# The RMS norm between two expert layers on 128x3 root elements, and one group of weight maxima read earlier

## The chip, the cores and the metric

The kernel runs on one core of a Trainium2 chip. A core has a matrix engine (TensorE: PE in the profile, its weight loads are PEld), a vector engine (VectorE: DVE), an activation engine (ScalarE: ACT), GpSimd (POOL) and SyncE (SP), whose queue issues nearly all DMAs here. PE writes to PSUM, which has eight banks of 128 x 512 fp32. The metric is device time in microseconds (us); lower is better.

## The reference

```python
x = attention(q, k, v)                    # (4,8,576,64), blocks of 64, block-causal, softmax
x = x.transpose(0, 2, 1, 3).reshape(2304, 512)
h = x @ w_in                              # 512 -> 2048
x = softplus(h) @ w_out                   # 2048 -> 512      first expert layer
rms = sqrt(mean(x * x, axis=-1) + 1e-6)   # one number for each token
xn = x / rms * rms_g
g = xn @ w_gate                           # 512 -> 1536
out = (g * sigmoid(g) * (xn @ w_val)) @ w_out2   # second expert layer
```

Inputs and outputs are fp32. The change concerns `rms` and, apart from it, the largest magnitude of `w_gate`/`w_val`, which the kernel needs for a scale of its fp16 products.

## The kernel before, in words

**Layout.** The 2304 tokens are cut into NB = 6 blocks of BLK = 384. Activations are held transposed: features on the 128 partitions (KD = 4 groups of 128), tokens along the free axis. So the mean over a token's 512 features runs over partitions and over four groups.

**Stages.** Attention units (batch, query group, head pair) run for each block, and their PE work is mixed with the first expert layer (phase A: `g1` and `g2` with hidden groups 0 to 8 of 16, for all blocks). The last attention work ends at about 350 us. Phase B (about 355 to 565 us) runs hidden groups 9 to 15 for all blocks in the order 4, 5, 0, 1, 2, 3 and, at the end of each block, `evac_b`: the four result banks are added to the partial result (line 1086), squared and summed over the four groups, and the norm's root is computed. Phase C (from 565 us) is the second expert layer: `g34` (gate and value products in seven fp16 block products, each in three passes) and `g5`.

**The root (lines 1088 to 1110).** ACT squares four tiles of 128x384, DVE adds them into `acc`. PE multiplies by a matrix of ones (line 1097), so that the token sums stand on every partition, 384 columns wide. From there all is 128x384: DVE scales the sums (line 1099); ACT loads a table set, takes Ln and then Exp with factor -0.5 (lines 1102 to 1104); the next activation loads its own set again. One Newton step on DVE follows, four operations (the three products in `pair2`, line 1080, and line 1109). The last two blocks evacuated (2 and 3 in token order; the fifth and the sixth below) are normalised at once (`direct`). The other four store the 128x384 root to DRAM (line 1114), and `load_xn` reads it back in phase C beside the block.

**The norm itself (`norm_x`).** DVE multiplies each of four tiles by `rms_g` and by the root `rs` (line 1126); then ACT and DVE split and combine quarters of the block into seven fp16 pairs (lines 1131, 1132, 1080).

**The maxima.** `top_unit` loads 512 KB of raw weights twice for each unit and DVE takes the largest magnitude of each (line 544). For the first eight gate/value units (16 loads, 8 MB) that happens before phase B's own weights are converted, after the seven units of w1 that phase B needs. `scales` turns maxima into a power of two with one small fp32 PE product of the form that spreads a column over all partitions (line 561: the column, broadcast, as weights; the identity `id_b` as the moving side) and some 128x1 DVE operations.

**What sets the order.** Nothing is scheduled at run time. `Plan` collects every operation with a key, an estimated duration and its dependences, simulates the engines twelve times, keeps the best round and emits all instructions in that order. Each engine then runs its queue in order; so does SP, where a load that waits for its buffer holds back every DMA behind it. Buffers come from rings: raw weights use `R_wraw` (two buffers) in attention and, from phase B's weights on, also `R_m` (two more). In attention SP's queue also carries the transposes of the probabilities (line 868, `pt<-pst`), which the product with V waits for.

Of the kernel before, what the change touches and what calls it, by code (L numbers as in the profile page):

```python
# [312 lines left out]
def t_mm16(n):  # L313
    return n * 0.4167e-3
# [46 lines left out]
def kernel(  # L361
# [71 lines left out]
    rs_dram = {j: dram.tile([128, BLK], FP32, name=f"rsd{j}") for j in range(NB)}  # L433
# [9 lines left out]
    R_r = Ring(pool_at(1), 3, [128, BLK], FP32, "r")  # L443
# [6 lines left out]
    def mm(o, l, r, start, stop, **kw):  # L450
        nc.tensor.matmul(o, lhsT=l, rhs=r, start=start, stop=stop, **kw)  # L451
# [60 lines left out]
    fac_b = R_fac.new()  # L512
    R_id = Ring(pool_at(1), 1, [128, 128], FP32, "id")
# [563 lines left out]
    rs_op = []  # L1077

# [3 lines left out]
    def evac_b(j, key, direct):  # L1082
# [23 lines left out]
        rs_op[:] = [op("ACT", 2 * t_act(BLK) + 2.56, key, root, [ms], [rs])]  # L1106
        pair2(key, t, rs, rs, ALU.mult, [rs], [t])
        pair2(key, t, t, ms, ALU.mult, [t, ms], [t])
        op("DVE", t_dve2(BLK), key, lambda: nc.vector.tensor_scalar(t(), t(), -0.5, 1.5, ALU.mult, ALU.add), [t], [t])
        pair2(key, rs, rs, t, ALU.mult, [rs, t], [rs])  # L1110
        if direct:
            norm_x(j, y, rs, key)
            return
        op("SP", 0.45, key, lambda: nc.sync.dma_start(out=rs_dram[j], in_=rs()), [rs], [("rsd", j)], done=1.0, nbytes=196608)


    def load_xn(j, key):
        t, rs = R_y.new(), R_r.new()
        load(key, t, y_dram[j], reads=[("yd", j, d) for d in range(KD)], writes=[(t, d) for d in range(KD)], nbytes=786432)
        load(key, rs, rs_dram[j], reads=[("rsd", j)], writes=[rs], nbytes=196608)  # L1120
        norm_x(j, t, rs, key)

    def norm_x(j, t, rs, key):
        x = x_b[j] = R_x.new()
        for k in range(KD):
            op("DVE", t_dve(BLK, True), key + 4, lambda k=k: nc.vector.scalar_tensor_tensor(t()[:, k], t()[:, k], gvec[:, k:k + 1], rs(), ALU.mult, ALU.mult), [(t, k), rs, "gvec"], [(t, k)], port=True)  # L1126
# [28 lines left out]
    def g34(j, i, key, first):  # L1155
# [41 lines left out]
        op("ACT", t_act(BLK, False) + 0.09 + (1.28 if first else 0.0), key + 2, lambda: nc.scalar.activation(e1(), ps(A)(), ACTF.Silu, scale=fac(3, sd)), [A, ("f", 3, sd)], [e1], after=rs_op + sp_op[-1:] if first else ())  # L1197
# [165 lines left out]
    R_fac.before = list(att_ops)  # L1363
    R_id.before = list(att_ops)
    op("DVE", 0.1, when(3 * per_block), lambda: nc.vector.memset(ones, 1.0), [], ["eye", "ones"])
    op("DVE", 0.1, win[NB - 1] - 6, lambda: nc.vector.memset(fac_b(), 0.0), [], [fac_b])
    load(win[NB - 1] - 6, id_b, eye, writes=[id_b], nbytes=65536)
    t_b = win[NB] + LAG * step
# [4 lines left out]
    for i in range(N_GV[0]):  # L1373
        top_unit(("gv", i), win[NB - 1] + 6 + 5 * (NF1 - NA) + 2 * i)
    scales(win[NB], 2, 0, scale_x)
    scales(win[NB], 0, 0, None)
# [146 lines left out]
```

## Time and profile before

| | us |
|---|---|
| time, median of 3 runs | 968.07 (964.41 to 977.81) |
| time of the profiled execution | 966.15 |
| its span | 964.4 |
| PE busy | 944.7 (98%) |
| PEld busy | 837.2 (87%) |
| DVE busy | 740.9 (77%) |
| ACT busy | 624.8 (65%) |
| DMA, mean | 156 GB/s, 150.83 MB |

The span runs from the first to the last instruction of the profiled execution; its time is 1.75 us longer. Busy time is the union of an engine's instructions, and a matmul's end is modelled, so for the cost of a matmul in a stream one reads the distance between starts, not its duration. An fp32 matmul stands in the trace as two passes, each with its own weight load. The granted TensorE clock is full speed (2.4 GHz) in every slice of the span.

### The profile page before, as it was taken

The numbers are of one execution on the slowest core, as the hardware profiler recorded it, in microseconds if no ns is written. First come the engines' busy times: TensorE is split into PE (matmuls) and PEld (weight loads), VectorE is DVE, ScalarE is ACT, GpSimd is POOL, SyncE is SP. The second block draws the span as 40 slices with busy tenths as digits, with TensorE's granted clock in tenths as the row PEclk, the third lists the DMA queues.
The fourth block names the chain that finished last, engine by engine and source line by source line (L and its number), as shares of the span: only waits on it lengthen the run. The fifth ranks groups of instructions, "written<-read, shape, count | busy, mean of one in ns | idle before, by whom it ended". The sixth has DMA issues, their size and how long they took to land. (4 is left out here: it accounts for less than half of the span.)

```text
span 964.4 us, 19849 instructions
## 1 busy us (share of the span) xinstructions
PE 944.7 (98%) x7592; PEld 837.2 (87%) x7592; DVE 740.9 (77%) x1689; ACT 624.8 (65%) x1406; POOL 51.4 (5%) x220
## 2 busy tenths in 40 slices
PE   7998999999999999999999999999999999999998
PEld 5797899999999999999999997777888778877885
DVE  6999998887988849579898789977877744455455
ACT  7999798886888859356898556545664633433332
POOL 1000211120121100000000000000000000000000
PEclk9999999999999999999999999999999999999999
DMA  8656767965667447977864751424130200135312
GB/s 281 189 163 203 195 161 165 221 166 152 157 150 153 108 152 251 366 272 290 284 224 161 239 164 31 153 109 165 47 110 1 78 22 13 56 129 184 136 67 88
DMA packets 128926, 150.83 MB, mean 156 GB/s; under 512 B 86464, under 2 KB 101312, under 8 KB 127296
## 3 DMA queue, kind: packets, MB, share of 16 engines
q1 hardware_dynamic: 128256, 143.29, 48.6%
q0 software_dynamic: 576, 6.29, 1.8%
q8 instruction: 59, 0.97, 0.4%
q14 instruction: 35, 0.29, 0.1%
HBM read 99.22 MB, written 29.88 MB: 134 GB/s over the span
## 5 line engine op out<-in xcount | busy, mean ns | idle before, releaser
L451 PE MATMUL b<-x,w 128*128 128x192 f16 (+1 forms) x4176 | 484.5, 272 | 3.3 <-ACT m L1188 3.3
L451 PEld LDWEIGHTS <-w 128*128 128x128 f16 x3024 | 250.6, 98 | 12.6 <-issue 4.4
L451 PE MATMUL b<-g,w 128*128 128x384 f32 x1152 | 227.9, 339 | 0.0
L451 PEld LDWEIGHTS b<-x,w 128*128 128x128 f32 x1152 | 200.2, 188 | 3.6 <-issue 0.6
L451 PEld LDWEIGHTS b<-g,w 128*128 128x128 f32 x1152 | 199.7, 188 | 2.5 <-issue 0.5
L451 PE MATMUL b<-w,g 128*128 128x512 f16 (+1 forms) x654 | 145.6, 377 | 0.0
L451 PEld LDWEIGHTS <-g 128*128 128x128 f16 x654 | 63.5, 98 | 67.8
L1176 DVE TENSOR_TENSOR m<-m 128x384 f32<-128x384 f32 x72 | 40.0, 555 | 74.7 <-ACT m L1188 73.8
L1188 ACT COPY m<-b 128x384 f32<-128x384 f32 x108 | 50.8, 477 | 69.0 <-PE b L451 68.5
L799 DVE TENSOR_REDUCE nm<-b 128x1 f32<-128x288 f32 (+8 forms) x160 | 70.4, 450 | 20.9 <-PE b L451 20.0
L836 ACT ACTIVATE P<-b,nm 128x288 f32<-128x288 f32 (+8 forms) x160 | 79.5, 499 | 6.4 <-DVE nm L799 4.0
L451 PE MATMUL b<-khl,qbd 128*128 128x448 f32 (+7 forms) x360 | 68.7, 310 | 1.1 <-DVE t L1030 0.8
L344 ACT CAST g<-t 128x384 fp32r<-128x384 f32 x96 | 48.9, 513 | 25.7 <-PE b L451 22.8
L862 DVE SCALAR_TENSOR_TENSOR pst<-P,nm,pst 128x64 f16<-128x64 f32 (+8 forms) x108 | 58.1, 544 | 4.4 <-ACT pst L859 3.7
L451 PEld LDWEIGHTS b<-khl,qbd 128*128 128x128 f32 x360 | 57.9, 188 | 3.4 <-DVE t L1030 1.1
L354 DVE TENSOR_TENSOR g<-t,g 128x384 fp32r<-128x384 f32 x96 | 52.6, 552 | 8.7 <-ACT g L344 8.6
L859 ACT ACTIVATE pst<-P,nm 128x576 f16<-128x576 f32 (+8 forms) x75 | 41.7, 569 | 9.9 <-DVE nm L845 5.3
L1197 ACT ACTIVATE t<-b,fac 128x384 f32<-128x384 f32 x36 | 20.9, 579 | 36.3 <-PE b L451 36.3
L844 POOL TENSOR_SCALAR nm<-nm 128x1 f32<-128x1 f32 (+1 forms) x120 | 31.8, 265 | 223.5 <-ACT P L836 167.0
L1212 ACT CAST g<-t 128x384 f16<-128x384 f32 x36 | 18.4, 511 | 36.8 <-DVE t L1211 36.8
L1174 DVE TENSOR_TENSOR m<-b,m 128x384 f32<-128x384 f32 x72 | 39.8, 553 | 2.3 <-PE b L451 2.3
L1023 ACT ACTIVATE t<-b 128x384 f32<-128x384 f32 x51 | 24.7, 487 | 25.3 <-PE b L451 23.7
(139 smaller groups left out, 1208.5 us busy)
## 6 DMA issues: line engine op xcount, KB each, us to landing
wraw<-in_w2gv_dram SPq DMA_DIRECT2D x33, 512.0 KB, 4.1
wraw<-in_w_dram SPq DMA_DIRECT2D x25, 512.0 KB, 3.9
wraw<-in_w2o_dram SPq DMA_DIRECT2D x16, 512.0 KB, 4.8
qf<-in_qP_dram SPq DMA_DIRECT2D x42, 192.0 KB, 3.1
m<-in_w2gv_dram SPq DMA_DIRECT2D x15, 512.0 KB, 6.1
y<-yd SPq DMA_DIRECT2D x10, 768.0 KB, 6.4
xd<-x SPq DMA_DIRECT2D x32, 192.0 KB, 3.7
x<-xd POOLq DMA_DIRECT2D x4, 1536.0 KB, 8.4
```

Source lines behind the costliest of these rows:

```text
L344: "ACT": ("ACT", t_act(n), lambda: nc.scalar.copy(dst(), src())),
L354: "DVE": ("DVE", t_dve(n), lambda: nc.vector.tensor_tensor(dst(), a(), b(), ALU.subtract)),
L451: nc.tensor.matmul(o, lhsT=l, rhs=r, start=start, stop=stop, **kw)
L799: aop("DVE", t_dve(cn), key, lambda sp=sp, col=col, cn=cn: nc.vector.tensor_reduce(nm()[:, col:col + 1], sp()[:, :cn], axis=AX.X, op=ALU.m ...
L836: aop("ACT", 0.24 + cn * 0.836e-3, key, lambda sp=sp, col=col, c0=c0, cn=cn: nc.scalar.activation(P()[:, c0:c0 + cn], sp()[:, :cn], ACTF.E ...
L844: small(("POOL",), lambda e: e.tensor_scalar(nm()[:, 4 + i0:4 + i1], nm()[:, 4 + i0:4 + i1], 1e-9, 1.0 if whole(u) else 2.0**-14, ALU.add, ...
L859: "ACT": ("ACT", t_act(n) + 0.09, lambda: nc.scalar.activation(hi(), pc(), ACTF.Copy, scale=r())),
L862: aop("DVE", t_dve(n, True), key, lambda: nc.vector.scalar_tensor_tensor(lo(), pc(), r(), hi(), ALU.mult, ALU.subtract), [P, (nm, "r", ib) ...
L1023: op("ACT", t_act(BLK, False) + (1.28 if not sp_op else 0.0), key - 5, lambda: nc.scalar.activation(e(), h()[:, :BLK], ACTF.Softplus), [h] ...
L1174: op("DVE", t_dve(BLK), k, lambda: nc.vector.tensor_tensor(dst(), a(), b(), alu), rd, wr, port=o_sb(rd))
L1176: op2([("DVE", t_dve(BLK), lambda: nc.vector.tensor_tensor(dst(), a(), b(), alu)), ("POOL", t_pool2(BLK), lambda: nc.gpsimd.tensor_tensor( ...
L1188: op("ACT", t_act(BLK, False), key + 1, lambda o=o, s=s: nc.scalar.copy(s(), ps(o)()), [o], [s])
```

## The change

1. **Token sums.** The product ones x `acc` (384 columns) becomes three products with `acc` as weights (128 tokens each) and one column of ones as the moving side. The sums then stand with tokens on partitions: 128 x 3 numbers for a block.
2. **Root.** On 128x3: a first guess by integer shift (DVE) and subtraction from a constant (one small ACT operation), then three Newton steps of three DVE operations each. No Ln, Exp or table load is left. The results of all blocks stay in one small tile, `rt`.
3. **Spread.** `norm_x` has PE spread the roots: three products of the form of line 561, into a PSUM bank, and DVE's four multiplications read the root from that bank. The store and reload of the root through DRAM are gone.
4. **Maxima.** The first eight gate/value units are loaded and reduced during attention, gated on `g1` products of blocks 2 to 4, in the two `R_wraw` buffers; the two scales that follow are due earlier.
5. The first Silu no longer has to come after the last root; ring `R_r` shrinks from 3 to 2 buffers.

```diff
-        op("PE", 0.65, key, lambda: mm(o()[:, :BLK], ones, acc(), True, True), [acc, "ones"], [o], cols=t_mm16(2 * BLK))
-        ms, rs, t = R_r.new(), R_r.new(), R_r.new()
-        op("DVE", t_dve(BLK), key, lambda: nc.vector.tensor_scalar(ms(), o()[:, :BLK], 1.0 / DM, 1e-6, ALU.mult, ALU.add), [o], [ms])
-        def root():
-            nc.scalar.preload_act_table_set("natural_log_exp_and_others")
-            nc.scalar.activation(rs(), ms(), ACTF.Ln)
-            nc.scalar.activation(rs(), rs(), ACTF.Exp, scale=-0.5)
...
+        def sums():
+            for c in range(NT):
+                mm(o()[:, c:c + 1], acc()[:, 128 * c:128 * c + 128], ones[:, 0:1], True, True)
+        op("PE", 0.25 * NT, key, sums, [acc, "ones"], [o], cols=t_mm16(128))
+        root(j, o, key)
...
+        dve(lambda: v.tensor_scalar(m(), o()[:, 0:NT], 1.0 / DM, 1e-6, ALU.mult, ALU.add), [o], ["rm"])
+        dve(lambda: v.tensor_scalar(t().bitcast(U32), m().bitcast(U32), 1, None, ALU.logical_shift_right), ["rm"], ["rt"])
+        op("ACT", 0.1, key, lambda: nc.scalar.activation(y().bitcast(I32), t().bitcast(U32), ACTF.Copy, scale=-1.0, bias=float(0x5F3759DF)), ["rt", rt_b], [cell])
+        for _ in range(3):
+            dve(lambda: v.scalar_tensor_tensor(t(), y(), -0.5, m(), ALU.mult, ALU.mult), [cell, "rm"], ["rt"])
+            dve(lambda: v.tensor_tensor(t(), t(), y(), ALU.mult), ["rt", cell], ["rt"])
+            dve(lambda: v.scalar_tensor_tensor(y(), t(), 1.5, y(), ALU.add, ALU.mult), ["rt", cell], [cell])
...
+        def spread():
+            for c in range(NT):
+                mm(o()[:, 128 * c:128 * c + 128], rt_b()[:, 3 * j + c:3 * j + c + 1].to_broadcast([128, 128]), id_b(), True, True)
+        op("PE", 0.109 * NT, key + 3, spread, [("root", j), id_b, rt_b] + [(t, k) for k in range(KD)], [o], cols=t_mm16(2 * BLK))
...
+    for i in range(N_GV[0]):
+        top_unit(("gv", i), win[3] + (win[NB] - win[3]) * i / N_GV[0], [[g1_op[steps[20 + 3 * i]]], [g1_op[steps[21 + 3 * i]]]])
+    scales(win[NB - 1], 2, 0, scale_x)
+    scales(win[NB - 1], 0, 0, None)
```

**Order on PE, end of phase B.** First PE's queue around the fifth block's token sum, before (`g,w` are second-layer products of the first expert, `x,w` first-layer products; `r` is `acc`):

```order
L451 MATMUL b_7363<-g,w 128x384 x3
L451 MATMUL b_7370<-g,w 128x384 x3
L451 MATMUL b_7375<-r,ones 128x384
L451 MATMUL b_7381<-x,w 128x384 x12
L451 MATMUL b_7351<-g,w 128x384 x3
L451 MATMUL b_7359<-g,w 128x384 x3
```

And the same place after the change (`rt` holds the roots, `id` is the identity):

```order
L450 MATMUL b_7401<-ones,r 128x1 x3
L450 MATMUL b_7405<-g,w 128x384 x3
L450 MATMUL b_7411<-g,w 128x384 x3
L450 MATMUL b_7417<-x,w 128x384 x12
L450 MATMUL b_7390<-g,w 128x384 x3
L450 MATMUL b_7397<-g,w 128x384 x3
L450 MATMUL b_7456<-id,rt 128x128 x3
L450 MATMUL b_7405<-g,w 128x384 x3
```

The one product became three, and 24 matmuls later PE's own queue now holds three products that wait for the finished root; before, PE waited for no root directly.

**Order on DVE, same place, after the change.** DVE's queue in the second half of the fifth block's root, from the second Newton step on; rows of other work stand between (`g<-t,g` belongs to the first expert, `w<-wg,fac,w` and `wg<-wg` convert weights):

```order
L1120 TENSOR_TENSOR rt<-rt 128x3
L354 TENSOR_TENSOR g<-t,g 128x384
L1121 SCALAR_TENSOR_TENSOR rt<-rt 128x3
L589 SCALAR_TENSOR_TENSOR w<-wg,fac,w 128x256
L1119 SCALAR_TENSOR_TENSOR rt<-rt 128x3
L589 SCALAR_TENSOR_TENSOR w<-wg,fac,w 128x512
L1120 TENSOR_TENSOR rt<-rt 128x3
L354 TENSOR_TENSOR wg<-wg 128x2x128
L1121 SCALAR_TENSOR_TENSOR rt<-rt 128x3
```

The five operations of 128x384 that stood in this stretch before are gone, and eleven of 128x3 stand in their place, the last five of them between four pieces of other work.

**Order on SP, in attention, after the change.** SP's queue where the first maxima are loaded, block 2's attention (`xd` stores x, `yd` stores partial results, `qf` loads queries):

```order
L464 DMA wraw<-in_w2gv_dram 128x512
L1058 DMA yd_84<-y 128x384
L870 DMA_TRANSPOSE pt<-pst 128x8x128
L1066 DMA xd_79<-x 128x384 x2
L464 DMA wraw<-in_w2gv_dram 128x512
L1058 DMA yd_84<-y 128x384 x2
L464 DMA qf_110<-in_qP_dram 128x384
L870 DMA_TRANSPOSE pt<-pst 128x8x128
```

The two loads of `wraw` are new here: before, no weight load stood between the transposes of this stretch. Sixteen such loads now stand there.

## Rows read from the trace of the kernel before

**Rows 1.** The page: span, busy time of the engines.

```profile
span 964.4 us, 19849 instructions
PE 944.7 (98%) x7592; PEld 837.2 (87%) x7592; DVE 740.9 (77%) x1689; ACT 624.8 (65%) x1406; POOL 51.4 (5%) x220
```

**Rows 2.** Windows: stretch, length, PE, PEld, DVE, ACT, POOL busy, clock, DMA share, GB/s.

```profile
0.00:40.00 40.00, 32.37 (x273) 24.43 (x274) 30.69 (x83) 32.08 (x95) 4.03 (x27) 1.00 0.74 247
75.00:150.00 75.00, 70.74 (x559) 64.31 (x560) 70.11 (x205) 65.81 (x180) 13.37 (x50) 1.00 0.68 184
...
225.00:300.00 75.00, 75.00 (x610) 71.42 (x609) 65.59 (x195) 61.11 (x168) 11.52 (x49) 1.00 0.64 157
...
560.00:590.00 30.00, 28.00 (x261) 24.81 (x260) 24.39 (x61) 18.73 (x36) 0.00 (x0) 1.00 0.41 131
```

**Rows 3.** Windows again, shorter: one stretch of attention with a full DVE.

```profile
120.00:140.00 20.00, 20.00 (x148) 18.88 (x148) 18.84 (x51) 18.39 (x49) 3.54 (x15) 1.00 0.73 182
```

**Rows 4.** Waits of PE: for whom, us in total, times, longest.

```profile
PE b L451 <- ACT y L680: 4.4, 1, 4.4
PE b L451 <- ACT m L1188: 3.3, 4, 1.2
PE b L451 <- DVE t L1030: 3.0, 3, 1.5
...
PE b L451 <- DVE r L1080: 0.4, 1, 0.4
```

**Rows 5.** Timeline of PE, 548 to 625 us: start, length, instructions, [idle before, releaser].

```profile
553.04 2.24 PE L451 MATMUL b<-g,w 128*128 128x384 f32 x12
555.12 2.24 PE L451 MATMUL b<-x,w 128*128 128x384 f32 x12
...
577.08 0.91 PE L451 MATMUL b<-r,ones 128*128 128x384 f32 x2
577.83 2.14 PE L451 MATMUL b<-x,w 128*128 128x192 f16 x24
579.81 0.64 PE L451 MATMUL b<-id,fac 128*128 128x128 f32 x4
580.29 2.14 PE L451 MATMUL b<-x,w 128*128 128x192 f16 x24
583.26 3.13 PE L451 MATMUL b<-x,w 128*128 128x192 f16 x36 [0.83 <-ACT m L1188]
```

**Rows 6.** Groups by line and shape, PE and PEld: count, busy us, mean ns.

```profile
L451 PE MATMUL b<-ones,nm 128*64 128x64 f32 x144 | 6.2, 222 | 0.0
L451 PEld LDWEIGHTS b<-id,fac 128*128 128x128 f32 x10 | 1.6, 189 | 0.0
```

**Rows 7.** Timeline of ACT around the last root.

```profile
576.29 1.28 ACT L1102 ACT_TABLE_LOAD   x1
578.63 0.53 ACT L1103 ACTIVATE r<-r 128x384 f32<-128x384 f32 x1 [1.05 <-DVE r L1099]
579.18 0.52 ACT L1104 ACTIVATE r<-r 128x384 f32<-128x384 f32 x1
579.72 1.28 ACT L1197 ACT_TABLE_LOAD   x1
582.75 0.46 ACT L1188 COPY m<-b 128x384 f32<-128x384 f32 x1
```

**Rows 8.** Timeline of DVE: small operations in a chain, then a maximum.

```profile
389.45 0.17 DVE L570 RECIPROCAL fac<-fac 128x1 f32<-128x1 f32 x1
389.65 0.15 DVE L571 TENSOR_SCALAR fac<-fac 128x1 f32<-128x1 f32 x1
389.84 0.23 DVE L576 TENSOR_SCALAR tops<-tops,fac 128x4 f32<-128x4 f32 x1
389.98 0.68 DVE L544 TENSOR_REDUCE tops<-wraw 128x1 f32<-128x512 f32 x1
390.57 0.55 DVE L354 TENSOR_TENSOR g<-t,g 128x384 fp32r<-128x384 f32 x1
```

**Rows 9.** Timeline: one transpose of probabilities on SP, and the product that uses it.

```profile
190.10 1.25 SPq L868 DMA_TRANSPOSE pt<-pst  x1
197.14 0.53 PE L451 MATMUL b<-pt,vhl 128*64 128x192 f16 x12
```

**Rows 10.** DMA issues: count, KB each, median us to landing.

```profile
wraw<-in_w_dram SPq DMA_DIRECT2D x25, 512.0 KB, 3.9
pt<-pst SPq DMA_TRANSPOSE x36, 4.8
```

More of the change, by code (lines that the diff above doesn't have):

```diff
@@ L432 @@
     acc_dram = {j: dram.tile([128, BLK // 128, 512], FP32, name=f"acd{j}") for j in range(NB)}
-    rs_dram = {j: dram.tile([128, BLK], FP32, name=f"rsd{j}") for j in range(NB)}
     R_x = Ring(com, 2, [128, KD, 2, BLK], F32R, "x")
@@ L442 @@
     R_wB = Ring(pool_b, NBF, [128, 2, 2, CW], F32R, "w")
-    R_r = Ring(pool_at(1), 3, [128, BLK], FP32, "r")
+    R_r = Ring(pool_at(1), 2, [128, BLK], FP32, "r")
     R_wg = Ring(pool_at(2), 2, [128, 2, CW], FP32, "wg")
@@ L512 @@
     fac_b = R_fac.new()
+    R_rt = Ring(pool_at(1), 1, [128, 3 * NB + 6], FP32, "rt")
+    rt_b = R_rt.new()
+    NT = BLK // 128
     R_id = Ring(pool_at(1), 1, [128, 128], FP32, "id")
@@ L1106, in evac_b @@
[L1106 to L1110, printed above, removed]
-        if direct:
-            norm_x(j, y, rs, key)
-            return
-        op("SP", 0.45, key, lambda: nc.sync.dma_start(out=rs_dram[j], in_=rs()), [rs], [("rsd", j)], done=1.0, nbytes=196608)
+        def sums():
+            for c in range(NT):
+                mm(o()[:, c:c + 1], acc()[:, 128 * c:128 * c + 128], ones[:, 0:1], True, True)
@@ new lines, in evac_b, with root, dve @@
+        op("PE", 0.25 * NT, key, sums, [acc, "ones"], [o], cols=t_mm16(128))
+        root(j, o, key)
+        if direct:
+            norm_x(j, y, key)
+    def root(j, o, key):
+        v, cell = nc.vector, ("root", j)
+        m, t = (lambda: rt_b()[:, 3 * NB:3 * NB + NT]), (lambda: rt_b()[:, 3 * NB + 3:3 * NB + 3 + NT])
+        y = lambda: rt_b()[:, 3 * j:3 * j + NT]
+        def dve(fn, reads, writes):
+            op("DVE", 0.07, key, fn, reads + [rt_b], writes)
+        dve(lambda: v.tensor_scalar(m(), o()[:, 0:NT], 1.0 / DM, 1e-6, ALU.mult, ALU.add), [o], ["rm"])
[5 more added lines that the diff above has]
+            dve(lambda: v.scalar_tensor_tensor(y(), t(), 1.5, y(), ALU.add, ALU.mult), ["rt", cell], [cell])
@@ L1117, in load_xn, with norm_x @@
     def load_xn(j, key):
-        t, rs = R_y.new(), R_r.new()
+        t = R_y.new()
         load(key, t, y_dram[j], reads=[("yd", j, d) for d in range(KD)], writes=[(t, d) for d in range(KD)], nbytes=786432)
-        load(key, rs, rs_dram[j], reads=[("rsd", j)], writes=[rs], nbytes=196608)
-        norm_x(j, t, rs, key)
-    def norm_x(j, t, rs, key):
+        norm_x(j, t, key)
+    def norm_x(j, t, key):
         x = x_b[j] = R_x.new()
+        o = R_a.new()
+        def spread():
+            for c in range(NT):
+                mm(o()[:, 128 * c:128 * c + 128], rt_b()[:, 3 * j + c:3 * j + c + 1].to_broadcast([128, 128]), id_b(), True, True)
+        op("PE", 0.109 * NT, key + 3, spread, [("root", j), id_b, rt_b] + [(t, k) for k in range(KD)], [o], cols=t_mm16(2 * BLK))
@@ L1196, in g34 @@
         e1 = R_t.new()
-        op("ACT", t_act(BLK, False) + 0.09 + (1.28 if first else 0.0), key + 2, lambda: nc.scalar.activation(e1(), ps(A)(), ACTF.Silu, scale=fac(3, sd)), [A, ("f", 3, sd)], [e1], after=rs_op + sp_op[-1:] if first else ())
+        op("ACT", t_act(BLK, False) + 0.09 + (1.28 if first else 0.0), key + 2, lambda: nc.scalar.activation(e1(), ps(A)(), ACTF.Silu, scale=fac(3, sd)), [A, ("f", 3, sd)], [e1], after=sp_op[-1:] if first else ())
         val1, gate2 = R_t.new(), s7
@@ L1363 @@
     R_fac.before = list(att_ops)
+    R_rt.before = list(att_ops)
     R_id.before = list(att_ops)
@@ L1366 @@
     op("DVE", 0.1, win[NB - 1] - 6, lambda: nc.vector.memset(fac_b(), 0.0), [], [fac_b])
+    op("DVE", 0.1, win[NB - 1] - 6, lambda: nc.vector.memset(rt_b(), 1.0), [], [rt_b])
     load(win[NB - 1] - 6, id_b, eye, writes=[id_b], nbytes=65536)
+    for i in range(N_GV[0]):
+        top_unit(("gv", i), win[3] + (win[NB] - win[3]) * i / N_GV[0], [[g1_op[steps[20 + 3 * i]]], [g1_op[steps[21 + 3 * i]]]])
+    scales(win[NB - 1], 2, 0, scale_x)
+    scales(win[NB - 1], 0, 0, None)
     t_b = win[NB] + LAG * step
@@ L1372 @@
         w_unit(("w1", f), R_wB, win[NB - 1] + 6 + 5 * i)
[L1373 to L1376, printed above, removed]
     order = [NB - 2, NB - 1] + list(range(NB - 2))
```

3 lines of the change are left out of this document (1 added, 2 removed).

## The prediction

> **What bounds the kernel now.** I read the page's busy times first, then the windows by stage, then who PE waits for, then PE's timeline. PE is busy 944.7 of 964.4 us [rows 1], and the windows show where the missing 19.7 us are: 7.6 in the first 40 us, 4.3 between 75 and 150 us, 2.0 between 560 and 590 us, and nothing in a stretch such as 225 to 300 us [rows 2]. A busy PE need not be a PE at its pace, so I checked the pace: in phase B twelve matmuls of 384 columns start 2.08 us after the twelve before (553.04 to 555.12), 0.173 us each [rows 5], and 384 columns at the 2.4 GHz that the clock column shows (1.00) are 0.160 us. There is little air inside a matmul. So this kernel is a PE queue with few holes: time changes by PE work added or removed, and by holes opened or closed. Work taken from ACT or DVE counts only where it closes a hole. All holes together are 2.0% of the span, and the largest named one, 4.4 us at the start [rows 4], is not touched.
>
> **The PE work.** Six blocks each lose one product and get six.
> Removed: ones x `acc`, two passes of 384 columns. The next matmul starts 0.75 us after it (577.08 to 577.83) [rows 5].
> Added, spread: three products of the very form that the trace has as `id,fac`. Two such products, four passes, hold PE from 579.81 to 580.29, so a pass is 0.12 us [rows 5]; three products are six passes, 0.72 us.
> Added, sums: three products with one moving column. The trace has no such shape. What remains of a pass is its weight load, now of `acc`, 128x128 fp32. From below: if loads hide behind neighbours, a pass costs what the 64-column ones cost, 6.2/144 = 0.043 us [rows 6], 0.26 us for six. From above: the recorded length of a 128x128 fp32 load, 0.189 us [rows 6], 1.13 us for six. I take the `id,fac` pass, 0.12 us, since its fp32 load of 128 columns is the same: 0.72 us.
> Per block 0.72 + 0.72 - 0.75 = +0.69 us, for six **+4.1 us**. With the low price of the sums it is 6 x 0.23 = 1.4. With 0.189 us for all twelve passes it is 6 x (2.27 - 0.75) = 9.1. This is on the path: the queue around these products is dense [rows 5].
>
> The Trainium skill speaks against the sums ("TensorE: Matmul & The Clock Gate", section "LDWEIGHTS (loading the stationary operand)"): a load costs its columns over 1.2 GHz, however little is done with it, 107 ns here. By that figure the two added parts cost an estimated 12 x 0.107 = 1.28 us and the sum would be +3.2 us instead of +4.1. The 0.12 us pass of the trace agrees with it nearly.
>
> **ACT and DVE of the root.** ACT loses, for each block, two table loads of 1.28 us and Ln and Exp of 0.5 us [rows 7], and gets one 128x3 operation. DVE loses five 128x384 operations and gets eleven of 128x3. None of it is bound by these engines, except in two holes: PE waits 0.83 us at 583.26 for an ACT copy that began at 582.75 [rows 5, 7], behind the last root's two table loads; and 0.4 us once for the sum of squares [rows 4]. The first must go, since only Silu's own table load remains ahead. The four waits for `m` total 3.3 us, the longest 1.2 [rows 4]; the other three have no table load of the root ahead of them. Gain between 0.8 us and 2.4 (0.8, 1.2 and 0.4); I take **-1.2 us**, the two that name the root's own work.
>
> **A new wait.** The fifth block's spread stands 24 matmuls behind its sums in PE's queue, 24 x 0.173 = 4.2 us. The root must be done by then, or every product behind it in the queue is late. The chain: operations on a few elements, each needing the last, start 0.19 to 0.20 us apart [rows 8]; eleven make 2.1 us. The trip to ACT and back adds about 0.6 (an estimate: three more such steps). In between DVE has about four larger pieces, 0.3 to 0.6 us each by the nearest starts (a 128x512 takes 0.59 to the next start [rows 8]), of which each fills a gap in the chain: net 1.4 us. PE's results reach DVE and back in two further steps, 0.4. Together 4.5 us against 4.2: **+0.3 us**, at least 0 and at most about 1 if ACT's operation queues behind an activation. The sixth block's spread stands 120 fp16 matmuls behind its sums; 24 of those take 1.98 us (577.83 to 579.81) [rows 5], so it has about 10 us and does not wait. The four blocks read back in phase C have their roots long before. There the spread holds one PSUM bank while DVE multiplies; three `g5` groups follow it on PE before the next gate products, and those take banks freed earlier, so I count nothing; without that cover it would be DVE's four multiplications, at most 0.59 us each (the 128x512 of [rows 8]), 2.4 us a block.
>
> **The maxima.** Sixteen reductions at 0.59 us [rows 8] put 9.4 us of DVE work into about 180 us of attention, where DVE was busy 65.6 of 75 us [rows 2]: 87% becomes 93%. From below: at 94% between 120 and 140 us PE had no hole [rows 3]. From above: in 75 to 150 us, at 93%, PE lost 4.3 of 75 us [rows 2], which over 180 us would be 10. That stretch holds the passage from the whole fp32 units to the split ones, which the later stretch does not have, so the first row is nearer. The loads also pass through SP's queue ahead of transposes. A transpose issued at 190.10 is used at 197.14, 7.0 us later [rows 9], and lands in 4.8 us (median) [rows 10]: about 2.2 us of margin in this tightest case. A 512 KB load takes 3.9 us to land [rows 10] but shares the engines, at a DMA share of 0.64 [rows 2]. Some margin is eaten; I take **+1.5 us** for both. The 8 MB that leave phase B leave a stretch where PE had no hole, so nothing is gained there.
>
> **The sum.** 964.4 + 4.1 - 1.2 + 0.3 + 1.5 = 969.1 us of span; with the 1.75 us between span and time, **970.9 us**. Its base is the profiled execution, 966.15 us, which lies 1.9 us under the median of 968.07 and inside the runs shown. It is 0.3% above that median.
>
> **Rivals.**
> *Holes close and sums hide.* All that could close closes (-2.4), the sums cost the low price (+1.4), attention costs nothing: 964.4 - 1.0 + 1.75 = 965.2 us. For it: weight loads overlap matmuls everywhere here. Against: three loads in a row with one column between them have nothing to hide behind.
> *Weight loads in series.* If fp32 loads did not overlap the matmul before, a spread pass would cost 0.189 for the load and about 0.125 for 128 columns (a third of the removed product's 0.375 us pass [rows 5]), a sums pass 0.189: six of each, 3.0 us, +2.3 a block, +13.6 in all, 980.4 us with the other terms. The Trainium skill has this rule ("TensorE: Matmul & The Clock Gate", section "Part 3: Packing small matmuls — row/col tiling"): a load overlaps a running matmul only in another row group. Against it stands the trace: four loads of 0.189 us fit into 0.48 us [rows 5, 6].
> *Transposes late (the other side).* Place: SP's queue in attention. Each of 16 loads pushes a transpose past its margin, PE stands before the product with V. The sum without the attention term is 969.4 us; 2% over the median is 987.4; so it decides once each load costs (987.4 - 969.4)/16 = 1.1 us of PE. With the full 3.9 us less 2.2 of margin, 1.7 us each, it is 27 us, 997 us. For it: the margin above. Against: only the short 128x8x128 transposes are that tight; PE's queue holds expert products between.
> *Faster by more than 2%* would need all 19.7 us of holes, and most are at the start and the end.
>
> **How the numbers follow.** The forecast 0.65 (966 to 977 us, PE term within its bounds), holes and hiding 0.20, series 0.07, late transposes 0.06, faster by over 2% 0.02. The range must hold 8 in 10: it takes the forecast and the most of the second, and upward the forecast's own bounds (PE +9.1 instead of +4.1 gives 975.9, and 3 us more in attention 979): 964 to 979 us. About 2% is what a measurement of this kernel can tell from no change; only the late transposes cross it upward: faster 0.02, same 0.92, slower 0.06.
>
> **What would show it.** PE's busy time should rise by about 4 us (1.4 to 9.1), with starts 0.75 us apart around a group of sums or a spread; the wait for `m` near 583 us should be gone; a PE wait on `rt` should be under 1 us, once. In 160 to 340 us PE's busy time should stay full; a PE wait on `pt` or on DVE there, above 5 us in total, would make the attention step wrong. A PE busy time below 944 us would make the main term wrong.

## The result, and the profile after

| | before | after |
|---|---|---|
| time, median (22 runs each, side by side) | 967.6 us (964.41 to 977.81) | 973.71 us (970.43 to 976.77) |
| ratio, 95% interval | | 1.0065 (1.0054 to 1.0076) |
| profiled execution: time, span | 966.15, 964.4 | 976.77, 975.0 |
| PE busy | 944.7 | 955.8 |

The change costs 6.1 us by the medians, 0.65% by the ratio: within 2%, on the slow side. The forecast, 970.9 us, lies 3.3 us over this median of before and 2.8 us under what was measured. The profiled execution is the longest of the 22 that gave the median, so its +10.6 us of span shows the kinds of loss, not their usual size. The mean clock shows that the loss is not of this one execution alone: none of the 22 executions of the changed kernel lies above 0.998, while 51 of the 91 of the kernel before that ran beside the experiments have 1.000.

The page after, beside [rows 1]:

```profile
span 975.0 us, 19961 instructions
PE 955.8 (98%) x7652; PEld 850.3 (87%) x7652; DVE 731.3 (75%) x1721; ACT 610.2 (63%) x1394; POOL 52.9 (5%) x220
```

PE gained 11.1 us of busy time, and the holes stayed at 19 us (975.0 - 955.8 = 19.2, against 19.7). DVE and ACT lost 9.6 and 14.6 us of busy time, and the time did not fall with them. The windows after, columns as in [rows 2] (stretch, length, busy PE, PEld, DVE, ACT, POOL, granted clock, DMA share, GB/s):

```profile
0.00:40.00 40.00, 33.78 (x274) 26.01 (x275) 27.66 (x73) 33.05 (x101) 4.42 (x27) 0.96 0.68 234
75.00:100.00 25.00, 21.63 (x158) 18.47 (x156) 23.16 (x65) 21.56 (x53) 2.03 (x6) 0.93 0.54 165
150.00:360.00 210.00, 209.23 (x1673) 199.27 (x1670) 180.25 (x519) 166.06 (x439) 31.47 (x131) 1.00 0.82 202
...
425.00:435.00 10.00, 7.10 (x39) 6.78 (x38) 9.16 (x18) 8.54 (x18) 0.00 (x0) 0.92 0.46 167
435.00:445.00 10.00, 10.00 (x46) 10.00 (x46) 9.32 (x31) 7.21 (x14) 0.00 (x0) 0.73 0.62 198
560.00:590.00 30.00, 30.00 (x255) 29.69 (x255) 23.25 (x56) 14.81 (x31) 0.00 (x0) 1.00 0.22 73
```

Read two columns together: PE's busy time and the clock, which had been 1.00 everywhere before. The transition, 560 to 590 us, is now full (28.00 before). Attention from 150 to 360 us lacks 0.8 us; before it was full. New is a hole of 2.9 us in 425 to 435 us, with the clock at 0.92 and then 0.73. A PE at half clock counts as busy, so this loss hides in the busy column. Worked out as (1 - clock) x length, 0 to 40 us loses 1.6 us, 75 to 100 us 1.8, and 425 to 445 us 0.8 + 2.7 = 3.5: 6.9 us together, and with some 4.3 us of added PE work (measured below) that is about the 11.1.

The waits of PE after, beside [rows 4]:

```profile
PE b L450 <- ACT y L682: 4.5, 1, 4.5
...
PE b L450 <- DVE r L1080: 2.9, 1, 2.9
```

The copies `m` no longer appear (3.3 us before). No wait for `rt` stands in the list either. The wait for the sum of squares, `r`, was 0.4 us, at the fifth block's sums (546.05), and is 2.9, at the first block's. PE's timeline at that place (start, length, instructions, [idle before, releaser]):

```profile
425.87 2.28 PE L450 MATMUL b<-x,w 128*128 128x384 f32 x12
427.99 2.28 PE L450 MATMUL b<-g,w 128*128 128x384 f32 x12
433.17 1.18 PE L450 MATMUL b<-ones,r 128*128 128x1 f32 x6 [2.90 <-DVE r L1080]
434.21 4.19 PE L450 MATMUL b<-x,w 128*128 128x384 f32 x12
438.19 3.23 PE L450 MATMUL b<-g,w 128*128 128x384 f32 x12
441.26 0.39 PE L450 MATMUL b<-id,fac 128*128 128x128 f32 x2
...
443.56 2.24 PE L450 MATMUL b<-g,w 128*128 128x384 f32 x12
445.64 2.24 PE L450 MATMUL b<-x,w 128*128 128x384 f32 x12
```

These are the first block's token sums in phase B. Twelve matmuls took 2.12 us before the wait (425.87 to 427.99). Behind it they take 3.98 us (434.21 to 438.19) and then 3.07; the six passes of the sums take 1.04 us, and 0.59 where the clock is full (466.44 to 467.03, below). Half speed thus adds 1.86 + 0.95 + 0.45 = 3.3 us to a wait of 2.9: 6.2 us at one place, in this execution.

### The profile page after: what moved, and what is told of

Its sections match the earlier page's. It is cut to its first block, busy times and chain, and to the rows that moved or that the text cites. A ratio compares the mean times of both kernels' runs of the same rounds, so it can differ in the third digit from the quotient of the medians.

```text
span 975.0 us, 19961 instructions
## 1 busy us (share of the span) xinstructions
PE 955.8 (98%) x7652; PEld 850.3 (87%) x7652; DVE 731.3 (75%) x1721; ACT 610.2 (63%) x1394; POOL 52.9 (5%) x220
## 4 chain that ended last, share of the span: by engine, by line
PE 55%; DMA 2%; DVE 1%; ACT 0%; issue 0%; DVEq 0%; SPq 0%; ACTq 0%
PE b L450 55%; DMA m<-in_w2gv_dram 1%; DMA wraw<-in_w2o_dram 1%; DMA yd<-y 1%; DVE wa L493 0%; DVE wg L494 0%; DVE w L589 0%; DVE wg L354 0%; DVE fac L546 0%; ACT w L588 0%; DVE g L354 0%; ACT wraw L491 0%; ACT wg L492 0%; ACT g L344 0%; ACT r L1091 0%
## 5 line engine op out<-in xcount | busy, mean ns | idle before, releaser
L450 PE MATMUL b<-g,w 128*128 128x384 f32 x1152 | 230.5, 342 | 1.0 <-DVE g L354 0.4
L450 PEld LDWEIGHTS b<-g,w 128*128 128x128 f32 x1152 | 202.3, 190 | 3.8 <-ACT g L344 0.7
L838 ACT ACTIVATE P<-b,nm 128x288 f32<-128x288 f32 (+8 forms) x160 | 79.7, 501 | 14.5 <-DVE nm L801 8.5
L861 ACT ACTIVATE pst<-P,nm 128x384 f16<-128x384 f32 (+7 forms) x72 | 42.1, 595 | 11.4 <-DVE nm L847 5.9
```

The lines of the kernel that those rows point to most:

```text
L838: aop("ACT", 0.24 + cn * 0.836e-3, key, lambda sp=sp, col=col, c0=c0, cn=cn: nc.scalar.activation(P()[:, c0:c0 + cn], sp()[:, :cn], ACTF.E ...
L861: "ACT": ("ACT", t_act(n) + 0.09, lambda: nc.scalar.activation(hi(), pc(), ACTF.Copy, scale=r())),
```

## The experiments

**Theory after the result.** The steady PE work is what was forecast. The surplus is the wait at the first sums with the half clock behind it, and the moved maxima make that wait. **Rivals:** one-column passes or spreads cost more than reckoned; the root's DVE chain is late; or any new order of the same work costs that much by chance.

### The two parts apart

One kernel is the kernel before with the norm part alone (sums, root, spread; maxima where they were); another has the maxima part alone. In short, the maxima part:

```diff
     for i in range(N_GV[0]):
-        top_unit(("gv", i), win[NB - 1] + 6 + 5 * (NF1 - NA) + 2 * i)
-    scales(win[NB], 2, 0, scale_x)
-    scales(win[NB], 0, 0, None)
+        top_unit(("gv", i), win[3] + (win[NB] - win[3]) * i / N_GV[0], [[g1_op[steps[20 + 3 * i]]], [g1_op[steps[21 + 3 * i]]]])
+    scales(win[NB - 1], 2, 0, scale_x)
+    scales(win[NB - 1], 0, 0, None)
```

> The kernel before with the norm's part alone: sums, root and spread as in the change; the maxima are loaded and reduced where they were. Theory 'PE work' (two groups of small products for one, about 0.74 us a block more, 4.4 us in all): 4 to 6 us over the kernel before, PE busy about 4 us more at full clock. Theory 'maxima in attention' (the loss comes from the loads and reductions that were moved): within 1 us of the kernel before. Theory 'order' (holes and dropped clock that any new plan brings): anywhere between -2 and +8 us, with the excess over 4 us matched by holes and by a mean clock under 1.

> The kernel before with the maxima's part alone: the first 16 maxima loaded and reduced during attention, the norm as before. Theory 'PE work': no matmul is added, so within 1 us of the kernel before. Theory 'maxima in attention': 4 to 6 us slower, with PE holes between 160 and 360 us. Theory 'order': -2 to +4 us, and what it loses stands in holes of PE and in stretches at half clock, not between 160 and 360 us.

Measured: the norm part 969.04 us against 967.59 (ratio 1.0014, 1.0001 to 1.0026), +1.4 us. The maxima part 970.55 us (1.0037, 1.0015 to 1.0059), +3.0 us by the medians and +3.6 by the ratio. The 4 to 6 us that the theory of PE work expected of the norm part did not come; it left out the holes that close. Of the maxima part's loss little stands between 160 and 360 us (0.8 us of PE); it stands behind a wait and at half clock, which is what the theory of order expected. With the maxima alone, PE's timeline has the old product ones x `acc` behind just such a wait:

```profile
438.60 1.65 PE L451 MATMUL b<-r,ones 128*128 128x384 f32 x2 [3.23 <-DVE r L1080]
439.47 4.62 PE L451 MATMUL b<-x,w 128*128 128x384 f32 x12
443.88 1.31 PE L451 MATMUL b<-g,w 128*128 128x384 f32 x5
```

So the hole needs neither the new sums nor the new root: the old product waits 3.23 us too, and twelve matmuls behind it take 4.41 us (this execution, 978.33 us, is the longest of its 12). With the norm alone the first sums start without a wait, and PE is full at full clock from 425 to 445 us:

```profile
428.36 0.72 PE L450 MATMUL b<-ones,r 128*128 128x1 f32 x6
```

The profiles of the runs below agree. Wherever the maxima are moved, the sums stand in their planned place and POOL issues the reload of x in phase B, PE waits near the first sums: 2.90 us in the changed kernel, 3.12 and 3.23 with the spread and the sums twice, 3.22 with the spread by transposes, 2.83 and 1.18 with the first attempt at the reload. With the maxima in their old place the first sums do not wait. The norm part's longest wait for `r` is 0.8 us, at 549.20 us. Its +1.4 us fits its own terms: +4.3 us of PE work less the 3.3 us of waits for `m`, and 0.4 us more at `r`; its interval, 0.1 to 2.5 us, would fit others too.

### What a new order alone is worth

The kernel before, with one constant of its planner changed, so that the same work stands in another order on every engine:

```diff
-            a = 0.15
+            a = 0.14
```

> The kernel before with one number of the planner changed (the damping of its rounds, 0.15 to 0.14): the same work, another order on every engine. Theory 'order': 1 to 4 us away from the kernel before, with holes at other places and maybe a clock under 1.00. Theories 'PE work' and 'maxima': within 1 us.

Measured: 969.3 us against 967.59 (1.0029, 1.0009 to 1.0049). This one new order of the same work cost 0.1 to 0.5%; how far other orders spread was not tried. A difference of 3 us between two plans is therefore no evidence for a mechanism by itself, and the loss has to be shown at a place.

### The price of the new products

Each spread issued twice, and in another kernel each set of sums issued twice, with the plan unchanged:

```diff
+                mm(o()[:, 128 * c:128 * c + 128], rt_b()[:, 3 * j + c:3 * j + c + 1].to_broadcast([128, 128]), id_b(), True, True)
...
+                mm(o()[:, c:c + 1], acc()[:, 128 * c:128 * c + 128], ones[:, 0:1], True, True)
```

> The changed kernel with each spread's three products issued twice into the same bank; the plan does not know, so every other instruction keeps its place. Theory 'PE work' (a spread costs PE 0.7 us and PE is the bound): 6 x 0.7 = 4.2 us over the changed kernel, 10.5 over the kernel before. Rival (PE has slack there, or fp32 weight loads run beside other work): 0 to 1 us over the changed kernel.

> The changed kernel with the sums' three products issued twice, every other instruction in its place. Theory 'PE work' (a pass with one moving column costs its weight load, 0.10 to 0.12 us): 6 x 6 x 0.11 = 4 us slower than the changed kernel. Rival (loads hide behind neighbours, 0.043 us a pass): 1.5 us slower. Rival (loads in series, 0.19 us): 6.8 us slower.

Measured: 979.23 us with the spread twice, against 967.59 (1.0131, 1.011 to 1.0152), and 981.2 us with the sums twice, against 966.71 (1.0154, 1.0129 to 1.0178). That is 11.6 and 14.5 us over the kernel before, 5.5 and 8.4 us more than the changed kernel's 6.1. The timelines give the price at its place. First the spread twice, then the sums twice:

```profile
586.88 1.53 PE L450 MATMUL b<-id,rt 128*128 128x128 f32 x12
588.25 2.14 PE L450 MATMUL b<-x,w 128*128 128x192 f16 x24
```

```profile
435.81 2.72 PE L450 MATMUL b<-ones,r 128*128 128x1 f32 x12 [3.23 <-DVE r L1080]
438.39 4.19 PE L450 MATMUL b<-x,w 128*128 128x384 f32 x12
...
470.89 1.40 PE L450 MATMUL b<-ones,r 128*128 128x1 f32 x12
472.15 2.33 PE L450 MATMUL b<-x,w 128*128 128x384 f32 x12
```

Twelve passes of the spread hold PE for 1.37 us and twelve of the sums for 1.26, that is 0.114 and 0.105 us a pass. The changed kernel with single sets, in fp32 and in fp16 surroundings:

```profile
466.44 0.72 PE L450 MATMUL b<-ones,r 128*128 128x1 f32 x6
467.03 2.36 PE L450 MATMUL b<-x,w 128*128 128x384 f32 x12
469.23 1.05 PE L450 MATMUL b<-g,w 128*128 128x384 f32 x5
...
589.57 0.86 PE L450 MATMUL b<-id,rt 128*128 128x128 f32 x6
590.26 2.14 PE L450 MATMUL b<-x,w 128*128 128x192 f16 x24
```

From the sums' start to the second group behind them is 2.79 us (466.44 to 469.23), where twelve matmuls alone take 2.12: 0.67 us for the sums. The spread takes 0.69. Doubling therefore adds 6 x 0.67 = 4.0 us of sums (1.26 against 0.59 to the next start) or 6 x 0.68 = 4.1 us of spread (1.37 against 0.69). The spread's 5.5 us is 1.4 us more, which five executions hardly tell from it (their interval is 4 us wide). The sums' 8.4 us is twice as much. By the time alone it would lie nearest the rival of loads in series, 6.8 us; the rows exclude that one, since the pass costs no more than 0.105 us (1.26 us at 470.89). Its first rows show a 3.23 us wait and the doubled sums standing in the half clock behind it (2.58 us to the next start). That the whole surplus of 4.4 us is clock was not separated.

### The first sums later

The changed kernel with the sums of the four stored blocks due 10 us later, so that PE does other products until the sum of squares is there:

```diff
-        op("PE", 0.25 * NT, key, sums,
+        op("PE", 0.25 * NT, key + (0 if direct else 10), sums,
```

> The changed kernel with the token sums of the four stored blocks due 10 us later in the plan, so that the first block's sums stand some 8 us further back in PE's queue; same work. Theory 'hole at the first sums' (about 3 us of PE waiting for the squares near 430 us, and the half clock that follows it): the hole is gone and the clock near 430 to 470 us is 1.00, 3 to 6 us faster than the changed kernel, 968 to 971 us. Rival 'DVE is behind by as much everywhere' (another product waits in the sums' place): within 1 us of the changed kernel, with a PE wait of about 3 us at another instruction there.

Measured: 969.12 us against 966.71 (1.0029, 1.0017 to 1.0041). Two thirds of a per cent have become one third. The first sums no longer wait, and the stretch is at its pace (this execution, 967.12 us, is the shortest of its 12):

```profile
432.92 2.28 PE L450 MATMUL b<-g,w 128*128 128x384 f32 x12
435.04 0.72 PE L450 MATMUL b<-ones,r 128*128 128x1 f32 x6
```

The next group starts at 435.62, and PE is busy all of 430 to 470 us at a clock of 1.00. Since a new order alone may bring some 3 us, this run is support, not yet proof.

### Why the sum of squares is late

The changed kernel's own rows lead back from the hole. The timeline of all engines, POOL's and SP's DMA issues among them:

```profile
411.50 0.68 POOL L1071 DMA_DIRECT2D x<-xd  x1 [67.26 <-PE b L450]
412.20 0.33 SPq L464 DMA_DIRECT2D m<-in_w2gv_dram  x1
...
422.12 0.66 ACT L491 ACTIVATE m<-m 128x512 int32<-128x512 uint32 x1 [8.14 <-DMA m<-in_w2gv_dram]
...
422.81 0.69 DVE L493 SCALAR_TENSOR_TENSOR wa<-m 128x512 uint32<-128x512 uint32 x1 [4.80 <-ACT m L491]
...
428.55 1.94 DVE L1086 TENSOR_TENSOR y<-b,y 128x384 f32<-128x384 f32 x4
```

A 512 KB weight load issued at 412.20 is there only at 422.1, 9.9 us later ([rows 10] has 3.9 us for such loads). ACT stands idle for 8.14 us before it, with a softplus copy behind it in its queue; DVE stands idle for 4.80 us, then works off conversions, and reaches the block's four additions at 428.55. The sum of squares is ready 4.6 us after that. Ahead of the late load stands a reload of x, 1536 KB, issued by POOL at 411.50. The kernel before has that reload too (at 407.31), and its loads are as late: the view of its DMA issues from 407.2 to 407.4 us (KB each, us to landing) has

```profile
m<-in_w2gv_dram SPq DMA_DIRECT2D x1, 512.0 KB, 10.7
```

There the late load fed a maximum, and the block's additions on DVE waited for nothing but PE:

```profile
420.50 2.15 DVE L1086 TENSOR_TENSOR y<-b,y 128x384 f32<-128x384 f32 x4 [1.50 <-PE b L451]
```

So the late load is not new. What differs is what hangs on it. From 360 to 430 us, before and then after:

```profile
360.00:430.00 70.00, 70.00 (x401) 69.69 (x400) 52.34 (x104) 42.70 (x83) 0.68 (x1) 1.00 0.83 296
```

```profile
360.00:430.00 70.00, 70.00 (x402) 69.94 (x400) 61.73 (x121) 52.47 (x100) 0.68 (x1) 1.00 0.80 275
```

The DMA engines are nearly equally full (0.83 and 0.80). But before, 16 loads of this stretch fed maxima, one DVE operation each and no ACT work, beside 14 that were converted, and DVE had 17.7 us to spare. After, 8 feed maxima and 19 are converted: with the maxima gone, the planner pulls weight conversions forward into this stretch. That is 9.4 us more of DVE and 9.8 of ACT, each in a chain load, ACT, DVE that shares its queues with the first expert's activations and the block's additions. That the conversions let the late load reach the additions is read from these rows; no run held them back by themselves.

First attempt at the DMA's part: the first reload of x asked for three hidden groups later in the plan.

```diff
...
-            if f == NJ[j] and 0 < n and n + 1 < NB:
+            if f == NJ[j] and 1 < n and n + 1 < NB:
                 load_x(order[n + 1], key_b(s))
             g1(j, f, key_b(s), True)
+            if n == 1 and f == NJ[j] + 3:
+                load_x(order[n + 1], key_b(s), [g1_op[j, f]])
```

> The changed kernel with the first reload of x in phase B (1536 KB on POOL's queue) issued some three hidden groups (12 us) later; PE's order is the same but for 3 rows. Theory: that reload shares the DMA engines with the weight load whose late landing (412.20 to 422.1) put DVE behind, so without it the load lands in 4 to 6 us, PE's wait at the first sums falls from 2.9 us to under 0.5, the clock stays at full speed in 425 to 445 us, and the time falls by 3 to 6 us, to 0.1% to 0.3% over the kernel before. Rival: the DMA engines are full by the weight loads alone, so the load still takes 8 us or more, the wait stays over 2.5 us and the time stays at 0.6% over the kernel before.

Measured: 977.12 us against 966.84 (1.0106, 1.0085 to 1.0126), slower than the changed kernel; neither the theory nor the rival expected that.

The edit did not do what it was made for. A gate in the plan sets an order and no wait; POOL has nothing else in its queue there, so the reload went out at 409.67 as soon as its buffer was free, and ACT again stood idle for 8.14 us until the load behind it was there (420.39). What changed was the order on DVE and ACT, and PE got two waits there (2.8 us for `t` and 1.2 for `r`) with the clock at 0.74 in 425 to 445 us. It decides nothing between the two views of the reload; the hole again stands behind the late load.

Second attempt: the same reload, now issued by SP behind the first block's store of y. This is the only instruction that stands elsewhere than in the changed kernel; all other queues are the same row for row.

```diff
+    held = []
...
+        if j == 0:
+            held.append(x)
-        op("POOL", 1.04, key, lambda: nc.gpsimd.dma_start(out=x(), in_=x_dram[j]),
+        op("POOL", 1.04, key, lambda: None if j == 0 else nc.gpsimd.dma_start(out=x(), in_=x_dram[j]),
...
-            op("SP", 0.45, key, lambda: nc.sync.dma_start(out=y_dram[j], in_=y()),
+            def store():
+                nc.sync.dma_start(out=y_dram[j], in_=y())
+                if j == NB - 2:
+                    nc.sync.dma_start(out=held[0]().bitcast(FP32), in_=x_dram[0])
+            op("SP", 0.45, key, store,
```

> The changed kernel with one instruction in another place: the first reload of x in phase B (1536 KB) is issued by SP behind the first block's store of y, some 20 us later than by POOL; all other queues are the same, row for row. Theory: that reload shares the DMA engines with the weight load issued at 412.20 that landed 9.9 us later; without it the load lands in 4 to 6 us, PE's wait at the first sums (2.9 us) falls below 1 us, the granted clock stays at full speed in 425 to 445 us, and the time falls by 2.5 to 6 us, to 0.0% to 0.4% over the kernel before. Rival: the weight loads fill the DMA engines by themselves, the load still takes 8 us or more, the wait stays over 2.5 us with the half clock behind it, and the time stays 0.6% over the kernel before. In both, the later reload should land by 445 us, before the products that read it (about 447 us); if it doesn't, a new wait for x shows there.

Measured: 969.15 us against 966.61 (1.0024, 1.0012 to 1.0037), 4.0 us less than the changed kernel by the ratios. Its timeline, SP, ACT and PE (the longest of its 12 executions):

```profile
414.46 0.33 SPq L464 DMA_DIRECT2D m<-in_w2gv_dram  x1
...
419.33 0.68 ACT L491 ACTIVATE m<-m 128x512 int32<-128x512 uint32 x1 [3.09 <-DMA m<-in_w2gv_dram]
...
428.24 0.43 SPq L1102 DMA_DIRECT2D x<-xd  x1
...
428.78 2.28 PE L450 MATMUL b<-g,w 128*128 128x384 f32 x12
430.90 0.72 PE L450 MATMUL b<-ones,r 128*128 128x1 f32 x6
```

The load lands in 4.9 us (414.46 to 419.3) instead of 9.9, ACT's idle time falls from 8.14 to 3.09 us, and the first sums start without a wait; the clock is 1.00 from 425 to 470 us. The second block's sums wait 0.7 us instead. The reload, issued at 428.24 instead of 411.50, delays nothing that PE waits for. With no other instruction moved, sharing the DMA with that reload is shown as the cause of the late load, and the late load as the cause of the hole. The theory's load time, wait, clock and time all came within what was expected.

The Trainium skill ("DMA: Bandwidth & Descriptors", section "Queues, rings and completion order") says that each DMA engine takes turns between the queue rows that have work. POOL's reload and SP's loads are two such rows, and the 9.9 and 4.9 us agree with it. But two queues are not needed: in the last run the reload stands in SP's own queue, and a 512 KB load issued 1.8 us behind it (430.06) took 8.2 us to land. Whether the loads were held by turns or only by a lack of bandwidth, no run here separates.

### The spread in single passes

An fp32 matmul is two passes; a transpose of the broadcast column gives the same 128x128 spread in one.

```diff
-                mm(o()[:, 128 * c:128 * c + 128], rt_b()[:, 3 * j + c:3 * j + c + 1].to_broadcast([128, 128]), id_b(), True, True)
+                nc.tensor.transpose(o()[:, 128 * c:128 * c + 128], rt_b()[:, 3 * j + c:3 * j + c + 1].to_broadcast([128, 128]), id_b())
```

> The changed kernel with each spread made by PE transposes of the broadcast column (one pass each) in place of fp32 products (two passes each); every other instruction keeps its place. Theory 'PE work': three passes less in each of six spreads, 0.11 to 0.12 us each, about 2 us faster than the changed kernel, near 971.5 us. Rival (the spread is hidden): within 0.5 us of the changed kernel.

> The kernel before with the norm's part alone, and the spread made by transposes. Theory 'PE work': 2 us under the norm's part alone, so 967 us, the kernel before within 1 us. Rival (the spread is hidden): 969 us as the norm's part alone.

Measured: in the changed kernel 971.66 us (1.0057, 1.0035 to 1.008), which is not clear of the changed kernel's 1.0065; in the norm part alone 969.13 us (1.0024, 1.0006 to 1.0042, no better than with matmuls). So the 2 us do not show in the times. The product itself did what it should:

```profile
588.80 0.49 PE L1134 MATMUL b<-id,rt 128*128 128x128 f32 x3
589.13 2.14 PE L450 MATMUL b<-x,w 128*128 128x192 f16 x24
```

0.33 us a spread instead of 0.69, 6 x 0.36 = 2.2 us in all. In the norm part alone, the profiled execution (972.15 us, above its median) has a wait of 3.2 us for a maximum (`fac`, line 560) at 418.37, which the norm part's profile lacks. The plan is the same. DVE waited 5.22 us for a load there, issued just after the reload of x at 408.07, so that load can open a hole with the maxima in their old place too; how often it does is not known.

Both improvements together, on the changed kernel and on its norm part alone:

> The changed kernel with two edits together: the token sums of the four stored blocks due 10 us later (as in e5_sums_late, same order on every engine) and the spread as three single-pass transposes. Theory (the loss beside the steady PE work is the wait at the first sums with the half clock behind it): e5_sums_late's 2.4 us over the kernel before, less 6 x 0.36 us of the spread: +0.2 us over the kernel before, 0.9995 to 1.001, and 430 to 470 us full at clock 1.00. Rival (each change of order or timing costs 0 to 3 us by holes elsewhere, and the gain of single passes is eaten by them, as in e8_norm_only_transpose): no better than e5_sums_late, 1.003.

> The norm part alone (maxima in their old place), with the sums of the four stored blocks due 10 us later and the spread as transposes. Steady PE work over the kernel before: 6 x (0.67 + 0.33 - 0.65) = +2.1 us; the four waits for the copy m are gone, -3.3; no wait at the sums, -0.4. Theory: 1.6 us under the kernel before, ratio 0.998 to 0.9995, the first version under it. Rival (holes of a new order take what was won, as in e8_norm_only_transpose): 1.001 to 1.003.

Measured: the changed kernel with late sums and single passes 967.29 us against 966.84 (1.0004, 0.999 to 1.0019): as forecast, and no longer distinguishable from the kernel before. The norm part alone with both 969.51 us (1.0019, 1.0002 to 1.0036): forecast 0.998 to 0.9995, and missed. Its profile has a clock of 0.96 in the first 40 us and a 1.1 us wait for `fac` ahead of 430 us, so the time is the one that its rival gave. No version beat the kernel before.

## Why the prediction was right or wrong

"Within 2%" and the range held; the number was 2.8 us low, and that it was so near is partly luck. Half of that, 1.4 us, is the base: the profiled execution, 966.15 us, lay that much under the median of 967.6 that more runs gave. The other half is in the terms, where errors of both signs partly cancelled: the sum said +4.7 us, the steps below measure +5.8. Step by step:

**PE work, +4.1 us: right.** Measured 6 x (0.67 + 0.69 - 0.65) = +4.3. Three terms were off by little and cancelled. The sums cost 0.67 and the spread 0.69, not 0.72. The removed product cost 0.75 beside fp16 matmuls, where I read it, but 0.65 beside fp32 ones, where most of the six stood, as rows of the kernel before show that I had not read:

```profile
426.67 0.81 PE L451 MATMUL b<-r,ones 128*128 128x384 f32 x2
427.02 2.02 PE L451 MATMUL b<-x,w 128*128 128x384 f32 x9
428.88 2.24 PE L451 MATMUL b<-g,w 128*128 128x384 f32 x12
```

From 426.67 to 428.88 is 2.21 us; nine matmuls are 1.56 of it by [rows 5]. A distance of starts must be taken over the neighbour too, which here starts early and pays later. The choice of the `id,fac` pass for a shape that the trace lacked was sound: a one-column fp32 pass costs 0.105 us, nearly the 0.114 us of a 128-column one. The figure of the Trainium skill ("TensorE: Matmul & The Clock Gate", section "LDWEIGHTS (loading the stationary operand)"), 0.107 us a load, agrees with these rows. The forecast's own sign, PE busy up by 1.4 to 9.1 us, was passed all the same (+11.1), because matmuls at half clock count as busy.

**The rivals on PE work: excluded.** That holes close and sums hide was half right: the holes closed, but the sums cost 0.67 us and not 0.26. The rival of weight loads in series wanted 3.0 us for a spread and sums; they take 0.69 + 0.67 = 1.36. The rule of the Trainium skill behind it ("TensorE: Matmul & The Clock Gate", section "Part 3: Packing small matmuls — row/col tiling"), overlap only with another row group, is not borne out here.

**Holes, -1.2 us: the mechanism right in part, the size too small.** The term was 0.8 us for one wait for `m` and 0.4 for the wait for `r`. All four waits for `m` went, 3.3 us, also with the norm part alone, which is more than the 2.4 us that I set as the most. The 0.4 us for `r` went as well; the new 2.9 us stand at another block's sums. I let three waits for `m` stand because no table load lay ahead of them. ACT's rows of the kernel before show what lay ahead of the longest:

```profile
574.07 1.45 ACT L1091 ACTIVATE t<-y 128x384 f32<-128x384 f32 x3
575.43 0.84 ACT L1188 COPY m<-b 128x384 f32<-128x384 f32 x2
```

Squares of the last block stood ahead of two copies that PE waited for. After the change copies and squares alternate (squares at 578.64 and 579.07, a copy at 579.48, a square at 579.84, a copy at 580.26), and PE has other products. That looks like a matter of the new order, which was not tested by itself, and no term of mine held it.

**The new wait for `rt`, +0.3 us: not there.** The fifth block's spread starts on time:

```profile
559.65 1.21 PE L450 MATMUL b<-g,w 128*128 128x384 f32 x6
560.69 0.92 PE L450 MATMUL b<-id,rt 128*128 128x128 f32 x6
561.37 1.29 PE L450 MATMUL b<-g,w 128*128 128x384 f32 x6
```

The chain of small operations fitted under its 24 matmuls; the bound "at least 0" held.

**Maxima in attention, +1.5 us: 0.8 us** missing in 150 to 360 us; no wait for transposes over 1 us, so the rival of late transposes did not come.

**The step that failed** is the last sentence on the maxima: "The 8 MB that leave phase B leave a stretch where PE had no hole, so nothing is gained there." It asked only what PE could gain. It did not ask what would move into the place of what had left. Before, a load that landed 10.7 us after its issue fed a maximum, and the first block's additions ran as soon as PE let them (420.50); after, the planner had put conversions on ACT and DVE there, a late load held them up, and the first sums came 2.9 us late. The maxima part alone shows the hole, and moving one DMA out of its way closes it. The second gap of the same step is that no term stood for the clock: a wait was priced at its length, where behind this one PE lost another 3.3 us at half speed.

Put together, in us: +4.3 PE work, -3.3 waits for `m`, +0.8 attention, +4.0 (by the ratios of the kernel with the reload moved) for the hole and its clock, make 5.8 of the 6.1 measured. The sum came so near by luck: 3.1 us of surplus in its terms (holes that closed, waits that did not come) stood against the 4.0 that it did not see. This sum mixes sizes from single profiles with a difference of ratios whose intervals are some 2 us wide, so its closing to 0.3 us is no proof of each term. It leaves out the 0.4 us at `r` that closed, and the 0.7 us wait that came with the moved reload, by which the 4.0 is too small. The rest may be the pace below, or holes and half clock at 0 to 100 us, which differ from profile to profile; this stays open.

## What to carry to other kernels

When work leaves a stretch, ask what an order made by a planner will put there, and read that stretch's slack on the engines that feed the bound, not only the bound's own holes. Price a new wait of about 3 us on PE as the wait plus what the clock takes behind it, and look at the clock column beside the busy column, since a PE at half speed looks busy. When a gain or loss is as small as what a new order of the same work brings (0.1 to 0.5% in the one tried here), an edit that moves one instruction and leaves all other queues as they were shows a cause where a new plan cannot.

## What the hardware showed unexpectedly

**A wait of 2.9 us cost as much again.** Behind 2.90 us of idle PE twelve matmuls took 3.98 us instead of 2.12, at a granted clock of 0.73 in 435 to 445 us; 3.3 us were lost. Behind 3.23 us they took 4.41. Behind a wait of 0.68 us for `r` (second block, reload moved) they took 2.20. All seven profiled waits of 2.8 to 3.3 us between 415 and 440 us have half clock around or behind them. Near 2 us the length alone does not decide: in the kernel before, 2.01 us of idle PE ahead of 13.21 us left the clock at 1.00 (13.21 to 17.21 us); in the changed kernel, behind 2.03 us of idle PE ahead of 80.04 us, it was 0.50 from 82.04 to 84.04 us. The granted clock is either 2.4 or 1.2 GHz; slices in between are means. Mean clock and time go together over executions of the changed kernel: 975.45 us at 0.993, 974.3 at 0.995, 973.2 at 0.996, 971.46 at 0.998 (medians of 3, 7, 9 and 3).

**Two exact paces at full clock.** The same twelve fp32 matmuls start 2.12 us apart up to 428 us and 2.08 apart from 443.56 on, at a clock of 1.00 in both, and in phase B most switches stand at groups of small products (441.26 and 466.44 in the changed kernel). The changed kernel runs more of phase B at 2.12 than the kernel before. At 0.04 us a group of twelve and some 26 groups more, this is an estimated 1 us in all; what sets the pace was not tried.

**A reload doubled the landing beside it.** 512 KB took 9.9 us beside a 1536 KB reload and 4.9 without it; in the kernel before, 10.7 beside the same reload.
